# Attention and a Fourier mixer in one kernel on one core: the second product's additions spread over its pieces, forms of u in their own places, product with v behind the next step's scores

## The chip, the cores and the metric

The kernel runs on one core of a Trainium2 chip. A core has a matrix engine (TensorE, PE in the profile, with its weight loads listed as PEld), three engines for elementwise work (VectorE, DVE; ScalarE, ACT; GpSimd, POOL) and DMA queues, here issued by SyncE. Each engine works through its own queue of instructions, and semaphores tie the queues together. The metric is the device time of one launch in microseconds (us).

The profiler records one execution. Lines such as L1128 are lines of the kernel before; names such as `w_all` or `e` are those of its tiles.

## The reference

Two blocks follow each other. The first is attention with a threshold, for 8 batches of 8 heads, 576 rows, 64 columns a head:

```python
scores = scale * np.matmul(q, k.transpose(0, 1, 3, 2))
thresh = np.max(scores, axis=-1, keepdims=True) - tau
scores = np.where(scores >= thresh, scores, -1000000000.0)
scores = scores - np.max(scores, axis=-1, keepdims=True)
attn = np.exp(scores)
attn = attn / (np.sum(attn, axis=-1, keepdims=True) + 1e-09)
return np.matmul(attn, v)
```

The heads are put side by side, to x of 8 x 576 x 512, and the second block mixes it:

```python
mixed = np.real(np.fft.fft(np.fft.fft(x, axis=1), axis=2))
u = x + mixed
un = (u - mean(u)) / np.sqrt(var(u) + 1e-06)
ch = np.maximum(un @ w_ch1, 0.0) @ w_ch2        # 512 -> 2048 -> 512
return u + ch
```

Everything is float32.

## The kernel before

*Attention.* Two heads are handled together (a pair; 32 pairs in all, four to a batch). A pair takes five steps t = 0 to 4: four of 128 query rows for both heads and one for the 64 rows left over. In a step `scores` writes q times k to PSUM (tile `sc`, L427). `softmax` takes the negated row maximum on VectorE (L451), the exponential on ScalarE (L459), the threshold and the sum on VectorE (L467, then L472 and L481 on tiny columns) and normalizes one head's half of `e` on VectorE (L484) and the other on ScalarE (L488). In step t == 4 ScalarE then copies a corner of `e` (L497). One step later `weights_in_parts` transposes `e` on TensorE (`pe` at L530, `pw` at L548), and ScalarE copies the result to `e_t` (L550). `weighted_values` multiplies it with v (`pv`, L577), part 0 after step 2 and part 1 after the pair's last step.

*Mixing.* When the four pairs of a batch are there, `fold_rows` and `mixing` fold x by symmetry, go through two products with tables (`py` L680, `pa` and `pb` L697 to L705), and leave u, transposed, in `u_t`: L717 and L718 on VectorE, L720 and L724 on GpSimd.

*The two large products.* The 4608 rows are cut into nine groups of 512. Group 0 runs as plain products. Groups 1 to 8 run in `two_level`, which computes both products with Strassen-like schemes: seven products in place of eight, paid for with additions.
- The first product goes through four parts of seven products each, in the order `ORDER`. Its right operands are quarters of u or forms of them, t1 to t3 and minus_t4, each a subtraction of GpSimd (`u_form`, L997). Their four places come from the tile pool "u", which also holds the rows of u until the store of the result has read them.
- The second product applies the scheme on two levels. The outer loop runs over the seven products `L1`, the inner one over seven pieces `J`; each piece is four matmuls (eight records in the profile) into a bank (L1168), and after pieces 3 and 6 the bank is copied or added to a tile v_u, v_11, v_22, v_21 or v_12 (L1198, L1200, L1203). `l1_form` (L1090) and `l2_forms` (L1110) build the left operands one product ahead, on VectorE and GpSimd. At the end of outer product 7, one GpSimd addition (L1216, 128 x 1792) adds v_u to v_22 and v_21; `gather` (L1128) combines the seven columns of each by six calls; `finish` (L789) scales by 1/std and adds to u; then the rows are stored (L796). In this version all of that is emitted at one place, between two products. v_12 follows in the same manner after outer product 3, the last.

*Order of the work.* TensorE runs in the order of the program text. For the other engines, from the third batch on, the scheduler of the language orders the instructions. The main loop (L1490) goes through the attention steps: the scores of step i, then the transposes of step i-1 in two parts with `fill()` around them, then `softmax(i)`, then `fill()`, then `weighted_values`. `fill` draws one piece of mixing and as many pieces of the products as a budget of matmul columns allows; a group is a generator, and each `yield` ends a piece.

Of the kernel before, what the change touches and what calls it, by code (L numbers as in the profile page):

```python
# [9 lines left out]
FP32 = mybir.dt.float32  # L10
INT32 = mybir.dt.int32
UINT32 = mybir.dt.uint32
ALU = mybir.AluOpType
# [34 lines left out]
def kernel(  # L48
# [12 lines left out]
    nc = tc.nc  # L61
    B, H, S, D = q.shape
# [3 lines left out]
    NPAIR = H // 2  # L66
    NT = 5
    ND = DM // 128
# [9 lines left out]
    NG = B * S // BT  # L78
    RING = 2 * S

    const = ctx.enter_context(tc.tile_pool(name="const", bufs=1))
    sb = ctx.enter_context(tc.tile_pool(name="sb", bufs=2))
# [756 lines left out]

    ORDER = (1, 5, 2, 6, 4, 7, 3)
    L1 = (1, 2, 5, 4, 6, 7, 3)
    J = (1, 2, 5, 4, 6, 7, 3)
    HH = HID // 2
# [120 lines left out]
    s1_tile = w1[3]  # L966
    l2_room = [w2_all[:, 512 * n : 512 * (n + 1)] for n in range(6)]
    l2_at = 0
    NV = 7 * 128
    v_u, v_11, v_22, v_21, v_12 = (  # L970
        w2_all[:, 3072 + NV * n : 3072 + NV * (n + 1)] for n in range(5)
# [3 lines left out]
    def two_level(g, rows):  # L975
        forms = w2_forms() if g == 1 else iter(())

        def tokens(k, n):
# [6 lines left out]
            )  # L985

        b = {(k, n): tokens(k, n) for k in range(2) for n in range(2)}
        t1, t2, t3, minus_t4 = (
            sb.tile([128, 512], FP32, tag="u", bufs=4, name=f"t_u{m}")[:, :].rearrange(
                "p (c two n) -> p c two n", c=2, two=2  # L990
            )
            for m in range(4)
        )

        def u_form(out_, in0, in1):
# [30 lines left out]
        for part in range(4):  # L1026
# [4 lines left out]
            for at, m in enumerate(ORDER):  # L1031
# [37 lines left out]
                else:  # L1069
                    add(h01, bank[:, :])  # L1070
                    relu(h01, part == 3)
                next(forms, None)
                yield 4096
            if g > 1:
                s1_part(part)
        for _ in forms:
            pass
        if g == 1:
            for part in range(4):
                s1_part(part)  # L1080
# [4 lines left out]
        lefts = {}  # L1085

        def l1_form(out_, in0, in1, engines):
            for n, eng in enumerate(engines):
                c = slice(512 * n, 512 * n + 512)
                eng.tensor_tensor(out=out_[:, c], in0=in0[:, c], in1=in1[:, c], op=ALU.subtract)  # L1090

        def l2_forms(m):

# [16 lines left out]
                eng.tensor_tensor(out=out_, in0=in0, in1=in1, op=op)  # L1110
                yield

        def gather(eng, v, n):

            v = v.rearrange("p (v j n) -> p v j n", v=n, n=128)

            def at(first, count, step=1):
                return v[:, :, first : first + step * (count - 1) + 1 : step]

            def one(j, count):  # L1120
                base = v[:, :, j]
                return bass.AP(
                    tensor=base.tensor, offset=base.offset,
                    ap=[list(base.ap[0]), list(base.ap[1]), [0, count], [1, 128]],
                )

            def plus(to, other):
                eng.tensor_tensor(out=to, in0=to, in1=other, op=ALU.add)  # L1128

            for k in range(n):  # L1130
                w = v[:, k]
                p1 = bass.AP(
                    tensor=w.tensor, offset=w.offset, ap=[list(w.ap[0]), [0, 2], [1, 128]]
                )
                plus(w[:, 1:5:3], p1)
            plus(at(5, 1), at(4, 1))
            plus(at(6, 1), at(2, 1))
            plus(at(6, 1), at(4, 1))
            for k in range(n):
                w = v[:, k]  # L1140
                u3 = w[:, 5]
                u3 = bass.AP(
                    tensor=u3.tensor, offset=u3.offset, ap=[list(u3.ap[0]), [0, 2], [1, 128]]
                )
                plus(w[:, 2:4], u3)

        def finish(i, n, v):
            v = v.rearrange("p (j n) -> p j n", n=128)
            cols = slice(256 * n, 256 * n + 256)
            rows.add(2 * i, cols, v[:, 1:7:5])  # L1150
            second = v[:, 3:4]
            rows.add(2 * i + 1, cols, bass.AP(
                tensor=second.tensor, offset=second.offset,
                ap=[list(second.ap[0]), [-128, 2], [1, 128]],
            ))

        for _ in l2_forms(1):
            pass
        P, V = nc.gpsimd, nc.vector
        for at, m in enumerate(L1):  # L1160
            banks = []
            for jn, j in enumerate(J):
                if jn in (0, 4):
                    banks.append(ps.tile([128, 512], FP32, tag="mm", bufs=4, name="po"))
                to = banks[-1][:, 128 * (jn % 4) : 128 * (jn % 4 + 1)]
                right_ = block(g, True, 7 * at + jn)
                for s in range(4):
                    nc.tensor.matmul(  # L1168
                        to, lefts[m][j][:, s], right_[:, 128 * s : 128 * (s + 1)],
                        start=jn in (0, 4) and s == 0, stop=s == 3, skip_group_check=True,  # L1170
                    )
                if jn == 0:
                    if m == 4:
                        l1_form(s1_tile, s1_tile, a11, (V, P, V, P))
                    if m == 6:
                        l1_form(a12, a12, s1_tile, (V, P, V, P))
                    if at < 6:
                        coming = l2_forms(L1[at + 1])
                        next(coming)
                        next(coming)  # L1180
                    if m == 2:
                        l1_form(a21, a11, a21, (P, P, P, P))
                if jn in (2, 4) and at < 6:
                    next(coming)
                if jn == 3 and m in (2, 5, 4, 6):
                    rows.load({2: 2, 5: 3, 4: 0, 6: 1}[m])
                    if m == 6:
                        rows.factors()
                    yield ND * 128
                if jn in (3, 6):  # L1190
                    size = 512 if jn == 3 else NV - 512
                    src = banks[-1][:, 0:size]

                    def here(v):
                        return v[:, 0:512] if jn == 3 else v[:, 512:NV]

                    if m in (1, 5, 4):
                        nc.scalar.copy(here({1: v_u, 5: v_22, 4: v_21}[m]), src)  # L1198
                    elif m == 2:
                        V.tensor_tensor(out=here(v_11), in0=here(v_u), in1=src, op=ALU.add)  # L1200
                    else:
                        to = here(v_12 if m == 3 else v_u)
                        V.tensor_tensor(out=to, in0=to, in1=src, op=ALU.add)  # L1203
                if jn < 6:
                    yield 2048
            if m == 2:
                gather(P, v_11, 1)
            elif m == 6:
                P.tensor_tensor(out=v_12, in0=v_u, in1=v_22, op=ALU.add)
                finish(0, 0, v_11)  # L1210
            elif m == 7:
                twice = bass.AP(
                    tensor=v_u.tensor, offset=v_u.offset, ap=[list(v_u.ap[0]), [0, 2], [1, NV]]
                )
                both = v_22_21.rearrange("p (v n) -> p v n", v=2)
                P.tensor_tensor(out=both, in0=both, in1=twice, op=ALU.add)  # L1216
                gather(V, v_22_21, 2)
                finish(1, 1, v_22)
                finish(1, 0, v_21)
                rows.store(2)  # L1220
                rows.store(3)
            elif m == 3:
                gather(V, v_12, 1)
                finish(0, 1, v_12)
                rows.store(0)
                rows.store(1)
            background()
            yield 2048

    def settle(b):  # L1230

# [152 lines left out]
    def fold_more():  # L1384
        if folds and next(folds[0], True):
            folds.pop(0)
# [100 lines left out]
    by_hand.close()  # L1487
    ctx.enter_context(tc.manual_schedule(engines={mybir.EngineType.PE}))

    for i in range(2 * per_batch, total + 1):  # L1490


        if i < total:
            scores(i)
        n, t = divmod(i, NT)
        if t > 2:
            fold_more()
        weights = weights_in_parts(i - 1)
        if t == 1:
            prep_ends(n)  # L1500
        if t == 2 and n + 1 < B * NPAIR:
            scale_q(n + 1)
        if t == 3 and n + 1 < B * NPAIR:
            prep_pair(n + 1)
        fill()
        next(weights, None)
        fill()
        next(weights, None)
        if i < total:
            softmax(i)  # L1510
        fill()
        if t == 2:
            weighted_values(n, 0)
        if t == 0:
            while folds:
                fold_more()
            weighted_values(n - 1, 1)
            folds.append(fold_rows(n - 1))
            if n % NPAIR == 0:
                while folds:  # L1520
                    fold_more()
            if n + 1 < B * NPAIR:
                load_v(n + 1)
        if i % per_batch == 0:
            start_batch(i // per_batch - 1)
    per_slot = cost(0) / 40
    while mixes or work:
        fill()
# [46 lines left out]
```

## Time and profile before

Three runs took 1689.12 to 1691.37 us, with a median of 1690.09 us. The profiled execution spans 1689.9 us.

| Stretch of the span, us | TensorE busy | VectorE busy | ScalarE busy | GpSimd busy | Granted clock |
|---|---|---|---|---|---|
| 320 to 510 | 182.7 of 190 | 116.4 | 79.4 | 108.9 | 0.98 |
| 510 to 695 | 171.2 of 185 | 135.5 | 93.6 | 82.5 | 0.96 |
| 880 to 1064 | 174.5 of 184 | 136.9 | 93.7 | 84.2 | 0.97 |
| 1248 to 1433 | 175.9 of 185 | 135.2 | 94.7 | 83.0 | 0.97 |
| 1433 to 1690 | 231.6 of 257 | 127.9 | 52.4 | 122.7 | 0.96 |

Between 510 and 1433 us attention of the later batches and the groups of products run side by side; after 1433 us only the last mixing and the last products are left. The granted clock is the share of full speed at which TensorE was let run. Costly groups of instructions around the change, as busy time and mean length:

| Line | Engine, shape | Count | Busy us | Mean ns |
|---|---|---|---|---|
| L1041 first product | PE, 128x256 | 1792 | 431.5 | 386 |
| L1168 second product | PE, 128x128 | 3136 | 420.8 | 277 to 288 |
| L467 | DVE, 128x576 | 288 | 228.8 | 812 |
| L1128 `gather` | DVE, 128x256 and others | 96 | 46.5 | 550 |
| L1128 `gather` | POOL, 128x128 and others | 40 | 31.3 | 814 |
| L789 `finish` | DVE, 128x256 | 64 | 44.3 | 739 |
| L1216 | POOL, 128x1792 | 8 | 31.9 | 3982 |
| L1209 | POOL, 128x896 | 8 | 17.8 | 2222 |
| L997 forms of u | POOL, 128x256 | 64 | 48.6 | 767 to 788 |

A wait is read as follows: an engine's instruction is ready in its queue, and the profile names the instruction on another engine, or in its own queue, that released it last. A mean over a group can hide several cases, so the places themselves have to be looked at in order of time.

### The profile page before, as it was taken

Reading aid. Unit: us, or ns where it says so; the run is one execution under the profiler, and the core shown is the slowest. Engines: PE = TensorE matmul, PEld = TensorE weight load, DVE = VectorE, ACT = ScalarE, POOL = GpSimd, SP = SyncE. Lnnn points to the kernel's source line nnn. Section 1 sums busy time; section 2 is a strip of 40 time slices with the busy share of each in tenths; the row PEclk is TensorE's granted clock in tenths of the full one; section 3 lists DMA queues with packets and bytes.
Section 4 is the critical chain, followed back from the end, with each engine's and each line's share of the span. In section 5 each row is a group of like instructions: output and inputs, shape, how many; then the busy total and the mean of one; then the engine's idle time right before and its main releaser. Section 6 shows DMA issues by size and latency. Waiting matters only on the chain. (4 is left out here: it accounts for less than half of the span.)

```text
span 1689.9 us, 27055 instructions
## 1 busy us (share of the span) xinstructions
PE 1570.3 (93%) x9770; PEld 1213.6 (72%) x9770; DVE 1178.3 (70%) x2438; ACT 794.6 (47%) x1700; POOL 856.6 (51%) x953
## 2 busy tenths in 40 slices
PE   8998888998998899989999999899998999989997
PEld 4555444555786778777787678777877777879897
DVE  7987886546676767777677767876778767625546
ACT  5865665433544465445545464546545554222121
POOL 6784666357452634543362534453453426336436
PEclk9999999999999999999999999999999999999999
DMA  6343332445553434525353435433363425436655
GB/s 168 107 110 127 98 106 63 140 151 173 171 186 120 125 112 144 179 83 159 109 169 116 141 114 165 159 121 115 106 193 108 130 98 175 165 116 238 217 182 199
DMA packets 245499, 239.05 MB, mean 141 GB/s; under 512 B 196947, under 2 KB 214869, under 8 KB 225014
## 3 DMA queue, kind: packets, MB, share of 16 engines
q1 hardware_dynamic: 242854, 237.02, 45.2%
q8 instruction: 78, 1.28, 0.3%
q10 hardware_dynamic: 2512, 0.30, 0.1%
q14 instruction: 55, 0.45, 0.1%
HBM read 207.50 MB, written 29.62 MB: 140 GB/s over the span
## 5 line engine op out<-in xcount | busy, mean ns | idle before, releaser
L459 ACT ACTIVATE e<-sc,neg 128x576 f32<-128x576 f32 x288 | 211.8, 736 | 249.8 <-DVE neg L451 249.6
L451 DVE TENSOR_REDUCE neg<-sc 128x1 f32<-128x576 f32 x288 | 207.1, 747 | 130.2 <-PE sc L427 98.0
L467 DVE SCALAR_TENSOR_TENSOR e<-sc,thr,e 128x576 f32<-128x576 f32 x288 | 228.8, 812 | 47.9 <-ACT thr L463 46.6
L1041 PE MATMUL ph<-t_u,w 128*128 128x256 f32 x1024 | 245.5, 386 | 9.6 <-POOL t_u L997 9.3
L1168 PE MATMUL po<-w,w_all 128*128 128x128 f32 x1792 | 242.1, 288 | 5.9 <-ACT ends L540 5.3
L1168 PEld LDWEIGHTS po<-w,w_all 128*128 128x128 f32 x1792 | 226.9, 203 | 15.3 <-issue 7.8
L1041 PEld LDWEIGHTS ph<-t_u,w 128*128 128x128 f32 x1024 | 188.7, 192 | 42.9 <-POOL t_u L997 11.3
L1110 POOL TENSOR_TENSOR w_all<-hs 128x512 f32<-128x512 f32 x72 | 100.3, 1395 | 225.4 <-PE po L1168 122.9
L427 PE MATMUL sc<-kT,qT 64*128 64x288 f32 x1024 | 177.3, 434 | 25.8 <-DVE e L467 24.8
L1041 PE MATMUL ph<-u_t,w 128*128 128x256 f32 x768 | 186.0, 387 | 6.3 <-ACT hs L1052 5.6
L1010 DVE TENSOR_TENSOR hs<-ph,hs 128x512 f32<-128x512 f32 (+1 forms) x128 | 105.0, 821 | 114.3 <-PE ph L1041 114.3
L548 PE MATMUL pw<-ident,e 128*128 128x128 f32 x1152 | 172.8, 277 | 6.2 <-ACT u L769 2.9
L1041 PEld LDWEIGHTS ph<-u_t,w 128*128 128x128 f32 x768 | 143.9, 193 | 34.5 <-issue 8.6
L427 PEld LDWEIGHTS sc<-kT,qT 64*128 64x128 f32 x1024 | 96.1, 187 | 93.1 <-issue 39.5
L550 ACT COPY e_t<-pw 128x512 f32<-128x512 f32 x256 | 147.7, 590 | 30.5 <-PE pw L548 29.7
L548 PEld LDWEIGHTS pw<-ident,e 128*128 128x128 f32 x1152 | 138.4, 143 | 23.5 <-issue 5.7
L1022 POOL TENSOR_TENSOR w<-hs 128x512 f32<-128x512 f32 x32 | 40.6, 1269 | 216.2 <-ACT hs L1018 205.8
L1168 PE MATMUL po<-w,hs 128*128 128x128 f32 x960 | 128.7, 281 | 0.0
L1168 PEld LDWEIGHTS po<-w,hs 128*128 128x128 f32 x960 | 119.2, 196 | 5.9 <-issue 5.5
L488 ACT ACTIVATE e<-e,den 128x576 f32<-128x576 f32 x96 | 74.5, 776 | 66.7 <-DVE den L481 66.4
L1018 ACT ACTIVATE hs<-hs 128x512 f32<-128x512 f32 (+1 forms) x80 | 60.7, 758 | 78.7 <-DVE hs L1010 77.9
L484 DVE TENSOR_SCALAR e<-e,den 128x576 f32<-128x576 f32 x120 | 89.6, 747 | 3.7
(203 smaller groups left out, 2758.0 us busy)
## 6 DMA issues: line engine op xcount, KB each, us to landing
w<-f SPq DMA_DIRECT2D x152, 1024.0 KB, 4.9
hs<-in_moe_w_ch_dram SPq DMA_DIRECT2D x23, 512.0 KB, 4.6
q_in<-in_q_dram SPq DMA_DIRECT2D x128, 72.0 KB, 2.3
out_dram<-u SPq DMA_DIRECT2D x36, 256.0 KB, 2.3
k_in<-in_k_dram SPq DMA_DIRECT2D x124, 72.0 KB, 2.4
v_in<-in_v_dram SPq DMA_DIRECT2D x64, 128.0 KB, 2.4
f<-w SPq DMA_DIRECT2D x14, 512.0 KB, 4.9
f<-w SPq DMA_DIRECT2D x7, 1024.0 KB, 4.3
```

Of the source, the lines that this page charges most:

```text
L427: nc.tensor.matmul(sc[j][:, c, 0:HALF], qT[hp, 128 * t : 128 * t + 128], kT[hp, k0 + HALF * c : k0 + HALF * (c + 1)], start=True, stop=True,)
L451: nc.vector.tensor_reduce(out=neg[:, j : j + 1], in_=sc[j][:, :, 0:HALF], axis=AXIS_XY, op=ALU.max, negate=True,)
L459: nc.scalar.activation(out=ej, in_=sc[j][:, :, 0:HALF], func=ACT.Exp, bias=neg[:, j : j + 1], scale=1.0)
L467: nc.vector.scalar_tensor_tensor(out=ej, in0=sc[j][:, :, 0:HALF], scalar=thr[:, j : j + 1], in1=ej, op0=ALU.is_ge, op1=ALU.mult, accum_out ...
L484: nc.vector.tensor_scalar(out=e[:, 0:S], in0=e[:, 0:S], scalar1=den[:, 0:1], scalar2=None, op0=ALU.mult)
L488: nc.scalar.activation(out=e[:, S : 2 * S], in_=e[:, S : 2 * S], func=ACT.Copy, scale=den[:, 1:2])
L548: nc.tensor.transpose(pw[:, c, :], e[:, c0 : c0 + 128], ident[:, :])
L550: nc.scalar.copy(e_t[:, 4 * j : 4 * j + 4, qs], pw[:, :, :])
L1010: nc.vector.tensor_tensor(out=to, in0=bank, in1=to if other is None else other, op=ALU.add)
L1041: nc.tensor.matmul(bank[:, 256 * q : 256 * q + 256].rearrange("p (two n) -> p two n", two=2), left[:, 256 * c + 128 * q : 256 * c + 128 * ...
L1110: eng.tensor_tensor(out=out_, in0=in0, in1=in1, op=op)
L1168: nc.tensor.matmul(to, lefts[m][j][:, s], right_[:, 128 * s : 128 * (s + 1)], start=jn in (0, 4) and s == 0, stop=s == 3, skip_group_check ...
```

## The change

Four things are altered.

1. *Additions spread over the pieces.* The calls of `gather`, `finish`, `l1_form` and `l2_forms` become lists of single jobs. A table `side` gives each a slot (outer product, piece), and one or two of them are emitted after that piece. The addition of v_u to v_22 and v_21 becomes two of 128 x 896, after the first two pieces of the last outer product, and `gather(V, v_22)` and its `finish` follow in that product's later slots. What belongs to v_12 and v_21 goes into a list `pending`; `tick` takes two jobs from it after every product of the next group's first product. The last group empties it at once. `gather` now takes one tile of seven columns at a time, five calls each.
2. *Forms of u in places of their own.* For groups after the first, t1 has a tile of its own, and t2, minus_t4 and t3 lie in places of `l2_room`, the room of the left operands. The pool "u" then holds only rows of u.
3. *The order of the first product* changes from 1, 5, 2, 6 to 1, 2, 5, 6, so that the first form is needed one product later.
4. *Product with v behind the next scores.* `weighted_values`, the folding that hangs on it, `load_v` and `start_batch` move from the end of a step to behind the scores of the next step, ahead of its transposes.

The aim is that no engine's queue holds a long run of additions in front of an instruction that TensorE waits for, and that TensorE has work at hand while ScalarE copies `e_t`.

```diff
-    ORDER = (1, 5, 2, 6, 4, 7, 3)
+    ORDER = (1, 2, 5, 6, 4, 7, 3)
...
+    t1_room = const.tile([128, 512], FP32, name="t1_room")
...
-        t1, t2, t3, minus_t4 = (
-            sb.tile([128, 512], FP32, tag="u", bufs=4, name=f"t_u{m}")[:, :].rearrange(
...
+        else:
+            rooms = [t1_room[:, :]] + [l2_room[(l2_at + m) % 6] for m in (4, 5, 0)]
+        t1, t2, minus_t4, t3 = (
+            room.rearrange("p (c two n) -> p c two n", c=2, two=2) for room in rooms
         )
...
                 next(forms, None)
+                tick()
                 yield 4096
...
+        while pending:
+            tick()
...
+        side = {}
+
+        def at_slots(at, slots, jobs):
+            for jn, job in zip(slots, jobs, strict=True):
+                side.setdefault((at, jn), []).append(job)
...
+            at_slots(at, (1, 2, 3, 5) if at == 3 else (0, 1, 3, 5), [next_form] * 4)
+        coming = {}
+        at_slots(1, (1, 2, 4, 6), l1_form(a21, a11, a21, (P, P, P, P)))
+        at_slots(2, (4, 5, 6), l1_form(s1_tile, s1_tile, a11, (V, P, V, P))[0:3])
+        at_slots(3, (0,), l1_form(s1_tile, s1_tile, a11, (V, P, V, P))[3:4])
+        at_slots(4, (1, 2, 4, 6), l1_form(a12, a12, s1_tile, (V, P, V, P)))
+        at_slots(2, (0, 1, 2, 3, 4), gather(P, v_11))
+        at_slots(4, (0, 2), finish(0, 0, v_11))
+        at_slots(
+            5, (0,), [lambda: P.tensor_tensor(out=v_12, in0=v_u, in1=v_22, op=ALU.add)]
+        )
+        at_slots(6, (0, 1), [plus(P, v_22, v_u), plus(P, v_21, v_u)])
+        at_slots(6, (2, 2, 3, 4, 4), gather(V, v_22))
+        at_slots(6, (5, 5), finish(1, 1, v_22))
...
+                for job in side.get((at, jn), ()):
+                    job()
...
-            elif m == 7:
...
-                P.tensor_tensor(out=both, in0=both, in1=twice, op=ALU.add)
-                gather(V, v_22_21, 2)
-                finish(1, 1, v_22)
-                finish(1, 0, v_21)
-                rows.store(2)
-                rows.store(3)
-            elif m == 3:
-                gather(V, v_12, 1)
-                finish(0, 1, v_12)
-                rows.store(0)
-                rows.store(1)
...
+        pending.extend(gather(V, v_12))
+        pending.extend(gather(V, v_21))
+        pending.extend(finish(0, 1, v_12))
+        pending.append(stores(0, 1))
+        pending.extend(finish(1, 0, v_21))
+        pending.append(stores(2, 3))
+        if g == NG - 1:
+            while pending:
+                tick()
...
+        for _ in range(2):
+            if pending:
+                pending.pop(0)()
...
-    for i in range(2 * per_batch, total + 1):
+    for i in range(2 * per_batch, total + 2):
...
+        if t == 3:
+            weighted_values(n, 0)
+        if t == 1:
+            while folds:
+                fold_more()
+            weighted_values(n - 1, 1)
+            folds.append(fold_rows(n - 1))
...
+        if i % per_batch == 1:
+            start_batch(i // per_batch - 1)
...
         if i < total:
             softmax(i)
         fill()
-        if t == 2:
-            weighted_values(n, 0)
-        if t == 0:
-            while folds:
-                fold_more()
-            weighted_values(n - 1, 1)
-            folds.append(fold_rows(n - 1))
...
-        if i % per_batch == 0:
-            start_batch(i // per_batch - 1)
```

## The prediction

> **What bounds the kernel now.** I read the page's busy shares first, then the waits of TensorE, the list of its gaps in the timeline, and the granted clock in narrow windows around them.
>
> ```profile
> PE 1570.3 (93%) x9770; PEld 1213.6 (72%) x9770; DVE 1178.3 (70%) x2438; ACT 794.6 (47%) x1700; POOL 856.6 (51%) x953
> ```
>
> TensorE is busy for 93% of the span, so what a reordering can win is in the 120 us in which it is not, and in the time in which it runs slowly. Its waits over the whole span:
>
> ```profile
> PE sc L427 <- DVE e L467: 24.8, 25, 2.4
> PE pe L530 <- ACT e L497: 20.0, 6, 3.5
> PE pv L577 <- ACT e_t L550: 11.2, 11, 1.3
> ...
> PE ph L1041 <- POOL t_u L997: 9.3, 2, 5.5
> ...
> PE pa L697 <- DVE tmp L718: 3.6, 5, 1.1
> ```
>
> The columns are the total, how often, and the longest. In the timeline these waits repeat at fixed places: from 510 us to 1433 us the kernel goes through five rounds of 184.5 us (20 attention steps and about one group of rows each), and every full round has the same gaps: 1.0 us at pv, 2.37 us and 1.31 us at sc, 1.29 us at pv, 3.25 to 3.39 us at pe, 0.55 us or more at pa; together 9.8 us. The pe gap at 933.8 us, in order of time:
>
> ```profile
> 925.69 4.00 POOL L1216 TENSOR_TENSOR w_all<-w_all 128x1792 f32<-128x1792 f32 x1 [2.05 <-DVE w_all L1203]
> 929.72 4.59 DVE L1128 TENSOR_TENSOR w_all<-w_all 128x256 f32<-128x256 f32 x7 [2.36 <-POOL w_all L1216]
> 934.23 2.19 DVE L789 SCALAR_TENSOR_TENSOR u<-w_all,rstd,u 128x256 f32<-128x256 f32 x4
> 936.35 0.51 DVE L484 TENSOR_SCALAR e<-e,den 128x576 f32<-128x576 f32 x1
> 936.89 0.24 ACT L497 COPY e<-e 128x64 f32<-128x64 f32 x1 [1.50 <-DVE e L484]
> 937.19 0.47 PE L530 MATMUL pe<-ident,e 128*128 128x128 f32 x1 [3.39 <-ACT e L497]
> ...
> 941.08 4.33 PE L1168 MATMUL po<-w,w_all 128*128 128x128 f32 x24
> ```
>
> The reader is to see that L484, half a microsecond of work, stands in VectorE's queue behind eleven instructions of the second product, and these behind a 4.0 us addition of GpSimd. The same windows, with the granted clock third from the right:
>
> ```profile
> 931.00:934.00 3.00, 2.80 (x24) 2.61 (x23) 3.00 (x6) 0.00 (x0) 3.00 (x5) 1.00 0.76 311
> 934.00:937.00 3.00, 0.00 (x0) 0.00 (x0) 3.00 (x7) 0.51 (x2) 0.96 (x2) 1.00 0.01 5
> 937.00:940.00 3.00, 2.26 (x10) 1.44 (x11) 3.00 (x7) 2.54 (x7) 1.37 (x2) 0.53 0.64 195
> 940.00:943.00 3.00, 3.00 (x14) 2.29 (x13) 2.90 (x7) 1.13 (x3) 3.00 (x6) 0.50 0.01 3
> 943.00:946.00 3.00, 3.00 (x23) 2.63 (x24) 1.18 (x2) 0.00 (x0) 3.00 (x5) 0.83 0.33 49
> 946.00:949.00 3.00, 3.00 (x24) 1.63 (x22) 2.97 (x7) 0.42 (x1) 2.24 (x5) 1.00 0.86 347
> ```
>
> The last gap costs twice: TensorE idles 3.4 us and then runs at half clock. Summed over windows of 4 us, the clock missing after each such gap is 3.4 us; the 2.37 us gap is followed by 1.7 us missing, the gaps of 1.3 us and less by none.
>
> **What the skill says.** "TensorE: Matmul & The Clock Gate", Part 1 (the HAM clock gate): the clock drops to half after an idle window of about 3.4 us and comes back after about 3.4 us of activity. The trace agrees: 0.50 to 0.53 after 3.39 us of idleness, for about 6.8 us. The same page, under the array's architectural detail: ScalarE and VectorE queues are strict FIFO. The L484 lines agree. "GPSIMD Engine Reference", Specifications: GpSimd shares its SBUF interfaces with VectorE, and two-input instructions contend. The trace agrees: the 128x512 addition of L1110 on VectorE takes 0.69 us alone and up to 1.75 us beside GpSimd's additions.
>
> **The change, part by part.**
>
> *Product with v behind the next scores.* No instruction is added. Ahead of the scores the pv matmuls wait for the copy L550; behind them the copy is 1.2 us of sc further on and more, so the waits of 11.2 us go: +11.2. What the swap risks: sc now issues earlier by the pv block, 2.3 us (part 0) or 2.84 us (part 1), and needs L467 of the step before to be done. From the timeline, the distance from the end of the last L467 to sc at eight such places of one round is 3.3, 4.0, 6.2, 0.6, 7.3, 4.6, 5.3 and 4.6 us. Only the 0.6 is short, and it comes from fold and mixing work (L610 to L670) that stood between two L467s; in the queue built for the changed kernel both L451s and both L467s come ahead of it. So the 1.31 us wait shrinks to about 0.2: 5 x 1.1 = +5.5. VectorE also gets its scores 2.3 us sooner before the 2.37 us wait. There its queue is full from 866 to 881 us, after 1.56 us idle waiting for those very scores; I let the earlier start take 1.2 us off the wait and 1.2 of the 1.7 us of missing clock: 4 rounds x 2.4 = +9.6.
>
> *Additions one or two per piece.* Per group VectorE had 12 instructions at L1128 (two columns of v together) and gets 15 of single columns; five of these took 1.37 us at the end of the kernel, where GpSimd was idle, and 2.77 us at 946 us beside it. Three sets are 4.1 to 8.3 us against 47.8/8 = 6.0 us now: nothing either way. GpSimd's 4.0 us L1216 becomes two additions of 128x896, which L1209 prices at 2.2 us each, and the first half is enough for the first set. Counting from the scores of the last step of a pair (921.9 us): v_u is complete at 0.65 (one piece earlier than now, by the built order), GpSimd's first half ends at about 2.8, five additions end at 4.2 to 5.5, one L789 0.5, L467 0.8, one L789 0.5, L717 and L718 0.9, two additions 0.6, L472 and L481 0.3, L484 0.5: 8.3 to 9.6, and with L497 8.6 to 10.0. TensorE needs it after its 1.1 + 9.9 us of matmuls in between, at 11.0. The gap closes; I leave 0.3. Gain: 5 rounds x (3.3 - 0.3 + 3.0 of clock) = +30. The sixth wait of this kind, at 1432 us, is another: L1110 waits there for GpSimd ahead of L484, and the built order keeps that. Likewise the 5.3 us at 510 us.
>
> *The new wait.* The remaining additions, two transposes, two L789, two L451 and two L467 of the next step follow in the same queue, and end at 15.9 to 17.3 on the same scale. The scores after next, no longer behind pv, want to start at 15.4. I take 1.2 us, and 0.5 us for waits that I don't see: 5 x 1.7 = -8.5.
>
> *Forms of u in their own places, order 1, 2, 5, 6.* Eight additions of 0.72 us per group on GpSimd stay. Their wait for the store of u (26.3 us of GpSimd, 7 times) goes, and t1 is needed third, not second. Elsewhere nothing waited for them; TensorE did twice, near the end. At 1581.85 us it waited 3.73 us for t1, while GpSimd was idle for the stores, and 1.7 us of clock are missing after it: t1 can now be early, and t2 and minus_t4, whose places are read until the group before ends, have two further products of 1.9 us of cover: +5.4. At 1479.29 us it waited 5.54 us for t1 too, but there GpSimd was busy from 1474.7 to 1484.1 us with the mixing additions (L720, L724) that make the tokens t1 needs; the change gives that one more product of cover, 1.9 us, and the half clock behind it likely stays: +1.9. Together +7.3. Product 6 now directly follows 5, whose ScalarE copy VectorE needs: hidden by the eight matmul records of 6 ahead of its own addition (1792 of L1041 in eight groups of 28 products; 431.5 us in all, so 1.9 us a product) against a copy of 0.58 us.
>
> *The end.* Seven L1128 and four L789 behind L1216 now partly run beside the last matmuls: +1.3.
>
> Sum: 11.2 + 5.5 + 9.6 + 30 - 8.5 + 7.3 + 1.3 = 56.4 us, 1634 us. The low end of each unknown (L484's gap closed but for 1 us: 5 x (2.3 + 3.0); nothing off the 2.37 us wait; 3.5 us of new waits per round; nothing at the end) gives 11.2 + 5.5 + 26.5 - 17.5 + 7.3 = 33, 1657 us; with every gap named closed, clock included, and no new wait it is 11.2 + 6.5 + 16.4 + 33.5 + 7.3 + 1.3 = 76, 1614 us. VectorE is busy for 137 of the 184.5 us of a round now and would be for 78% of it then, so I lean to the slow side of the middle: 1638 us.
>
> **The rivals.** *The wait moves* (1658 us): scores that issue earlier catch VectorE at the place I called the new wait for over 3 us, so that the half clock returns there: 5 x 6.5 instead of 8.5 lost, 56.4 - 24 = 32. For it: 15.9 to 17.3 against 15.4 is close. Against: of the other seven places six have 0.4 us or more to spare once the pv block is taken off, most of them 1.7 to 4.5. *VectorE sets the pace* (no change, 1688 us): its 137 us per round are spread so unevenly that each gap closed opens another. Against: from 945 to 1044 us no gap over 0.4 us shows, at the same work per step. *Slower* (1720 us): two half-clock gaps per round (2 x 6.5 = 13), as one-column additions contend with GpSimd in new places, and waits of 0.8 us at all eight swaps (6.4): 19.4 lost against 11.3 won per round (the 56.4, without the 8.6 from the forms and the end and without the new wait), 5 x 8.1 = 40, less the 8.6. For it: everything repeats five times, mistakes too. Against: the spare time just listed.
>
> **How the numbers follow.** Forecast 0.68, wait moves 0.17, no change 0.03, slower 0.12. Faster 0.85, same 0.03, slower 0.12. The range runs from 1612 us, all gaps closed, to 1676 us, past the first rival with one more such place; it leaves out most of no change and slower.
>
> **What would show it.** Right: no pv wait on L550; no pe wait over 1 us but the one near 1400 us; t_u waits gone; clock at 1.00 all through a round but for one place at most. Wrong: new sc waits on L467 over 2 us once per round, with 0.5 clock after them; L1125 (as the additions are then numbered) still ahead of L484 with GpSimd's addition before it.

## The result, and the profile after

Three runs of the changed kernel took 1715.66 to 1719.02 us, with a median of 1717.22 us: 1.0160 of the time before, 95% interval 1.0137 to 1.0183. It is slower by 27 us (1.6%), where 52 us less was forecast.

```profile
PE 1574.0 (92%) x9770; PEld 1215.3 (71%) x9770; DVE 1199.5 (70%) x2462; ACT 795.0 (46%) x1700; POOL 854.3 (50%) x961
```

TensorE does the same work in the same busy time (1570.3 us before); its idle time grew. Its waits over the whole span, with the lines of the changed kernel (L1045 and L1195 are the two products' matmuls, L1001 the forms of u, L1121 the forms of the second product, L1125 the additions of `gather`; `ph` and `po` are the PSUM banks of the two products, `pn`, L763, that in which u is transposed back):

```profile
PE pe L530 <- ACT e L497: 23.8, 8, 4.8
PE pa L697 <- DVE tmp L718: 21.8, 5, 4.7
...
PE sc L427 <- DVE e L467: 9.1, 16, 1.7
PE pn L763 <- ACT x L583: 6.2, 5, 1.3
...
PE po L1195 <- ACT w_all L1207: 4.9, 4, 1.3
```

The reader is to see three things. The waits that the change aimed at are gone: pv no longer waits for L550 (11.2 us before), and the scores wait 9.1 us in place of 24.8. Two waits on ScalarE's copies out of PSUM, 6.2 us at pn and 4.9 us at po, are new. And the rounds have two kinds of gap over 4 us, where before they had one of 3.3 us.

The places were found in order of time, as before. A round now takes 191 to 194 us, not 184.5. From the first pa gap (563.82 us) to the fifth (1331.06 us), four rounds, there are 767.2 us, against 738.2 us from pe gap to pe gap before. TensorE's busy time in them is 702.9 against 697.6 us, its idle time 64.4 against 40.6 us: 23.8 + 5.3 = 29 us. The two profiled spans differ by 24.9 us, so the loss arises in the rounds. In all four rounds together:

| Gap of TensorE, released by | before, us | after, us |
|---|---|---|
| sc, L467 on VectorE | 14.7 | 0.8 |
| pv, L550 on ScalarE | 9.2 | 0 |
| pe, L497 on ScalarE | 13.1 (one per round) | 20.3 (one per round, at another place; a rest of 0.55 at the old one in three) |
| pa, L718 on VectorE | 3.1 | 17.6 |
| pn, po, pw, py and ph, on copies and sums of ScalarE and VectorE | 0.5 | 25.7 |

The waits that went (sc and pv, 23.1 us) and the small ones that came (25.2 us) nearly cancel; the two long gaps make the rest.

The first new gap, at 945.7 us, in order of time; here and below only the instructions that bear on a gap are shown:

```profile
943.23 2.68 DVE L1125 TENSOR_TENSOR w_all<-w_all 128x128 f32<-128x128 f32 x4
944.60 0.40 ACT L713 COPY tmp<-pa 128x289 f32<-128x289 f32 x1 [1.01 <-POOL u_t L720]
945.83 0.87 DVE L789 SCALAR_TENSOR_TENSOR u<-w_all,rstd,u 128x256 f32<-128x256 f32 x2
946.62 1.14 DVE L1125 TENSOR_TENSOR w_all<-w_all 128x128 f32<-128x128 f32 x4
947.68 0.48 DVE L789 SCALAR_TENSOR_TENSOR u<-w_all,rstd,u 128x256 f32<-128x256 f32 x1
948.08 1.42 DVE L451 TENSOR_REDUCE neg<-sc 128x1 f32<-128x576 f32 x2
949.41 0.45 DVE L717 TENSOR_TENSOR tmp<-pa,tmp 128x289 f32<-128x289 f32 x1
949.78 0.45 DVE L718 TENSOR_TENSOR tmp<-pa,tmp 128x289 f32<-128x289 f32 x1
950.37 0.64 PE L697 MATMUL pa<-seq_even,y_e 128*1 128x145 f32 x2 [4.67 <-DVE tmp L718]
```

L484, which the change was to free, ran ahead of all this. But the mixing's L717 had its input at 945.0 us, when L713 ended, and stood in VectorE's queue until 949.4 us, behind additions and L789s of the second product and then two row maxima (L451). TensorE needs L718 behind it.

The second, at 890.4 us:

```profile
877.18 4.84 POOL L1125 TENSOR_TENSOR w_all<-w_all 128x256 f32<-128x256 f32 x5 [1.29 <-DVE w_all L1209]
...
888.72 1.73 POOL L387 TENSOR_SCALAR q_in<-q_in,q_scale 128x576 f32<-128x576 f32 x1
...
891.00 2.48 POOL L1121 TENSOR_TENSOR w_all<-w 128x512 f32<-128x512 f32 x2
892.29 1.73 DVE L1121 TENSOR_TENSOR w_all<-w_all,w 128x512 f32<-128x512 f32 x1 [6.69 <-POOL w_all L1121]
...
894.32 0.52 DVE L484 TENSOR_SCALAR e<-e,den 128x576 f32<-128x576 f32 x1
...
895.17 0.47 PE L530 MATMUL pe<-ident,e 128*128 128x128 f32 x1 [4.81 <-ACT e L497]
```

VectorE stood idle for 6.69 us: its next instruction was s2 of outer product 6, and GpSimd was late with s1, which s2 needs (s1 and s2 are left operands that `l2_forms` builds one after the other, s1 as a sum, s2 as s1 less another tile). L484, whose exponentials were done at 885.6 us (L467), stood behind s2, with the two tiny instructions that it needs, L472 and L481. The granted clock after the first gap, third from the right:

```profile
950.00:954.00 4.00, 3.63 (x15) 2.49 (x16) 3.23 (x10) 2.41 (x6) 4.00 (x6) 0.50 0.15 60
954.00:958.00 4.00, 4.00 (x27) 3.44 (x25) 0.69 (x1) 0.00 (x0) 4.00 (x7) 0.78 0.11 19
```

In windows of 1 us, the clock missing with each of the five pa gaps and four pe gaps of the rounds adds up to 3.4 us (5.1 us with one of them). Before, it was 3.4 us with five gaps of 3.3 us and 1.7 us with four of 2.4 us.

### The profile page after: what moved, and what is told of

The parts are those of the page before. It is cut to its first block, busy times and chain, and to the rows that moved or that the text cites. A ratio compares the mean times of both kernels' runs of the same rounds, so it can differ in the third digit from the quotient of the medians.

```text
span 1714.8 us, 27077 instructions
## 1 busy us (share of the span) xinstructions
PE 1574.0 (92%) x9770; PEld 1215.3 (71%) x9770; DVE 1199.5 (70%) x2462; ACT 795.0 (46%) x1700; POOL 854.3 (50%) x961
## 4 chain that ended last, share of the span: by engine, by line
PE 55%; DVE 24%; POOL 10%; ACT 5%; issue 4%; DMA 2%; SPq 0%; DVEq 0%; ACTq 0%; POOLq 0%
PE ph L1045 20%; PE po L1195 10%; PE pv L577 6%; PE sc L427 6%; PE pw L548 4%; DVE e L467 4%; DVE w_all L1125 3%; DVE neg L451 3%; PE po L821 3%; DVE w_all L1121 2%; POOL w_all L1125 2%; PE ph L803 2%; ACT e L459 2%; POOL w_all L1121 1%; DMA w<-f 1%
## 5 line engine op out<-in xcount | busy, mean ns | idle before, releaser
L459 ACT ACTIVATE e<-sc,neg 128x576 f32<-128x576 f32 x288 | 211.7, 735 | 277.5 <-DVE neg L451 277.2
L451 DVE TENSOR_REDUCE neg<-sc 128x1 f32<-128x576 f32 x288 | 206.3, 746 | 117.5 <-PE sc L427 98.3
L467 DVE SCALAR_TENSOR_TENSOR e<-sc,thr,e 128x576 f32<-128x576 f32 x288 | 228.9, 814 | 57.2 <-ACT thr L463 56.2
L1195 PE MATMUL po<-w,w_all 128*128 128x128 f32 x1792 | 246.7, 292 | 9.4 <-ACT w_all L1207 4.9
L1195 PEld LDWEIGHTS po<-w,w_all 128*128 128x128 f32 x1792 | 231.1, 207 | 21.6 <-issue 9.9
L1121 POOL TENSOR_TENSOR w_all<-hs 128x512 f32<-128x512 f32 x72 | 97.8, 1359 | 227.4 <-PE po L1195 152.2
L548 PE MATMUL pw<-ident,e 128*128 128x128 f32 x1152 | 174.0, 278 | 20.5 <-ACT ends L536 5.3
L1045 PE MATMUL ph<-u_t,w 128*128 128x256 f32 x768 | 181.5, 382 | 4.3 <-ACT x L583 1.9
L550 ACT COPY e_t<-pw 128x512 f32<-128x512 f32 x256 | 148.7, 593 | 49.2 <-PE pw L548 48.4
L548 PEld LDWEIGHTS pw<-ident,e 128*128 128x128 f32 x1152 | 137.4, 143 | 41.9 <-ACT ends L536 8.4
L1045 PEld LDWEIGHTS ph<-u_t,w 128*128 128x128 f32 x768 | 140.8, 190 | 30.8 <-issue 8.2
L1045 PE MATMUL ph<-w_all,w 128*128 128x256 f32 x672 | 158.6, 383 | 1.5 <-DVE hs L1014 1.5
L1045 PEld LDWEIGHTS ph<-w_all,w 128*128 128x128 f32 x672 | 123.1, 190 | 23.6 <-issue 5.8
L1195 PE MATMUL po<-w,hs 128*128 128x128 f32 x960 | 127.2, 279 | 1.9 <-ACT ends L536 1.4
L1195 PEld LDWEIGHTS po<-w,hs 128*128 128x128 f32 x960 | 117.5, 194 | 7.9 <-issue 5.1
L484 DVE TENSOR_SCALAR e<-e,den 128x576 f32<-128x576 f32 x120 | 90.2, 751 | 3.5
```

What stands on the lines that cost most here:

```text
L451: nc.vector.tensor_reduce(out=neg[:, j : j + 1], in_=sc[j][:, :, 0:HALF], axis=AXIS_XY, op=ALU.max, negate=True,)
L459: nc.scalar.activation(out=ej, in_=sc[j][:, :, 0:HALF], func=ACT.Exp, bias=neg[:, j : j + 1], scale=1.0)
L467: nc.vector.scalar_tensor_tensor(out=ej, in0=sc[j][:, :, 0:HALF], scalar=thr[:, j : j + 1], in1=ej, op0=ALU.is_ge, op1=ALU.mult, accum_out ...
L484: nc.vector.tensor_scalar(out=e[:, 0:S], in0=e[:, 0:S], scalar1=den[:, 0:1], scalar2=None, op0=ALU.mult)
L548: nc.tensor.transpose(pw[:, c, :], e[:, c0 : c0 + 128], ident[:, :])
L550: nc.scalar.copy(e_t[:, 4 * j : 4 * j + 4, qs], pw[:, :, :])
```

## The experiments

The first four runs set two theories against each other: 'additions', that the additions in their new slots make both long gaps, and 'swap', that scores issued earlier make them. From e5 on the theory is 'queue order': instructions that TensorE waits for stand, at two or three places per round, behind others in the queues of VectorE and ScalarE. Its rival is 'throughput': VectorE and GpSimd are short of time in these stages, so that a wait that is taken away turns up at the next place. Ratios are to the kernel before on the same chip, with their 95% intervals.

| Run | What it is | Median, us | Ratio |
|---|---|---|---|
| changed | all four alterations | 1717.2 | 1.0160 [1.0137, 1.0183] |
| e1 | before + swap of pv and scores | 1726.5 | 1.0195 [1.0175, 1.0215] |
| e2 | before + places of u and order | 1708.3 | 1.0086 [1.0066, 1.0107] |
| e12 | before + places of u, old order | 1707.1 | 1.0063 [1.0039, 1.0088] |
| e3 | changed - swap | 1709.3 | 1.0094 [1.0068, 1.0120] |
| e4 | changed - spread additions | 1755.4 | 1.0368 [1.0349, 1.0387] |
| e5 | changed, s1 on VectorE | 1689.3 | 0.9993 [0.9983, 1.0004] |
| e6 | changed, additions behind L718 | 1703.5 | 1.0078 [1.0063, 1.0093] |
| e7 | changed, both | 1672.9 | 0.9902 [0.9885, 0.9918] |
| e15 | e7 + one copy ahead | 1663.9 | 0.9845 [0.9830, 0.9860] |
| e8 | e3, additions behind L718 | 1706.8 | 1.0102 [1.0086, 1.0117] |
| e9 | e1 + copies ahead at every step | 1739.3 | 1.0257 [1.0239, 1.0275] |
| e10 | e9 + s1 on VectorE | 1735.7 | 1.0238 [1.0217, 1.0258] |
| e11 | e7 + copies ahead at every step | 1721.8 | 1.0150 [1.0131, 1.0169] |
| e13 | e1 + copy ahead at one step | 1735.3 | 1.0262 [1.0245, 1.0280] |
| e14 | e13 + s1 on VectorE | 1705.5 | 1.0085 [1.0069, 1.0101] |
| e16 | before + s1 on VectorE | 1684.7 | 0.9955 [0.9942, 0.9969] |
| e17 | e1, L789 behind L451 | 1711.9 | 1.0109 [1.0087, 1.0132] |
| e18 | e17 + s1 on VectorE | 1683.5 | 0.9942 [0.9920, 0.9963] |

### Which part loses

**e1, the swap alone.** The main loop of the changed kernel in the kernel before.

> The kernel before with the fourth alteration alone (product with v behind the next step's scores). Theory 'additions' (VectorE's and GpSimd's additions in their new slots stand ahead of L718 and L484 and make the two new gaps of 4 to 5 us): the pv waits on L550 (11.2 us) go, the pe gap of 3.3 us and its half clock stay, neither new gap appears; 1665 to 1680 us. Theory 'swap' (scores that issue earlier shift the attention steps against VectorE's other work, and this alone makes the new gaps): a gap over 4 us at pa or at pe in every round, 1700 us or more.

**e2, the places of u with the order 1, 2, 5, 6 alone; e12, the places with the old order.** The line in which e12 (+) differs from e2 (-):

```diff
-    ORDER = (1, 2, 5, 6, 4, 7, 3)
+    ORDER = (1, 5, 2, 6, 4, 7, 3)
```

> The kernel before with the forms of u in places of their own and the order 1, 2, 5, 6 alone. Both theories: no new gaps; t1 no longer waits for stores near 1582 us; 1680 to 1688 us.

> The second run (forms of u in their own places and order 1, 2, 5, 6; 1708 us) with the old order 1, 5, 2, 6: the places alone. If the order of the first product carries the loss of 15 us: 1680 to 1692 us. If the places do (GpSimd's forms run as soon as the tokens are there, and the scheduler orders VectorE's queue anew around them): 1700 to 1712 us.

**e3, the changed kernel with the main loop of before; e4, the changed kernel with the second product of before.**

> The changed kernel with the product with v put back to the end of the step: additions spread and forms of u stay. Theory 'additions': both gaps of 4 to 5 us stay and the pv waits come back, 1720 to 1735 us. Theory 'swap': the new gaps go and the pe gap stays closed, 1655 to 1675 us.

> The changed kernel with the additions of the second product put back into lumps between the products: swap and forms of u stay. Theory 'additions': the sum of the first two runs, 1660 to 1675 us, with the pe gap of 3.3 us once per round. Theory 'swap': as slow as the changed kernel or slower, 1705 us or more.

Measured: the swap alone loses 2.0%, the places with the order 0.9%, swap, places and order together 3.7%. 'Additions' had e1, e2 and e4 faster than the kernel before and falls. 'Swap' had e1 and e4 right, but not e3, where it expected both gaps gone and a time of 1655 to 1675 us; and neither theory had e2's loss. Putting the additions into slots, which 'additions' held guilty, is worth 2.0% on top of the other two (1.0368 to 1.0160), and nothing without the swap (1.0086 to 1.0094). The traces divide the gaps: the pa gap of 4.1 us is in e3, without the swap, and not in e1, so the spread additions make it; the pe gap of about 5 us is in e1 and e4, without the spread, and at most 2.3 us in the rounds of e3, so the swap makes it. In e1 the old pe gap stays too (2.9 us), and there is another, 4.1 us at py, in the place where pv stood:

```profile
919.23 2.46 POOL L1209 TENSOR_TENSOR w_all<-w_all 128x896 f32<-128x896 f32 x1 [2.50 <-DVE rstd L782]
919.67 2.69 DVE L789 SCALAR_TENSOR_TENSOR u<-w_all,rstd,u 128x256 f32<-128x256 f32 x2
922.29 1.41 DVE L451 TENSOR_REDUCE neg<-sc 128x1 f32<-128x576 f32 x2
923.11 1.28 ACT L459 ACT_TABLE_LOAD   x1 [3.47 <-DVE neg L451]
...
925.04 0.58 ACT L550 COPY e_t<-pw 128x512 f32<-128x512 f32 x1
925.67 0.56 PE L680 MATMUL py<-dim_c,f 128*48 128x65 f32 x3 [4.10 <-ACT e_t L550]
```

L550 had its input at 919.8 us. It stood in ScalarE's queue behind L459, L459 waited for L451, and L451 stood on VectorE behind two L789, slowed by GpSimd's L1209. Before the swap the same chain ended in the 1.29 us wait at pv.

The places of u seem to lose more than the order: 0.6% of the 0.9%, but the intervals of e2 and e12 overlap. In e2 the wait of the forms for the store is down from 26.3 us to 4.9 us. But VectorE's additions took longer. The group of `gather` on VectorE in e2:

```profile
L1132 DVE TENSOR_TENSOR w_all<-w_all 128x256 f32<-128x256 f32 (+1 forms) x96 | 59.4, 683 | 25.1 <-POOL w_all L1220 24.9
```

It was 46.5 us for the same 96 instructions, and VectorE's busy time as a whole rose from 1178.3 to 1217.8 us. A reading of this is that GpSimd, freed of the wait, now runs beside these additions and slows them; whether that or the scheduler's new order carries the loss was not tried.

### The two gaps of the changed kernel

**e5, s1 of outer product 6 on VectorE.**

```diff
-                (V if m == 1 else P, s1, x21, x22, ALU.add),
+                (V if m in (1, 6) else P, s1, x21, x22, ALU.add),
```

> The changed kernel, with one thing altered: the first addition of l2_forms for outer product 6 (s1, L1121) runs on VectorE, not on GpSimd, so that VectorE's next form s2 doesn't wait for GpSimd ahead of L484. Theory 'queue order': the pe gap of 4.5 to 4.8 us (four rounds) shrinks under 1.5 us and the half clock behind it goes, 4 x (3.3 + 3.4) = 27 us: 1685 to 1697 us; the pa gap on L718 stays. Rival 'throughput' (VectorE and GpSimd together are short of time in this stage, and TensorE meets the same lack at the next place): the gap turns up at po or sc with the same size, 1710 to 1720 us.

**e6, the additions of v_22 into the pending list, and that list behind the latest L718** (`issue_after` prescribes an order in one engine's queue and adds no wait for the result).

```diff
-        at_slots(6, (2, 2, 3, 4, 4), gather(V, v_22))
-        at_slots(6, (5, 5), finish(1, 1, v_22))
...
+        pending.extend(gather(V, v_22))
+        pending.extend(finish(1, 1, v_22))
...
-                pending.pop(0)()
+                with tc.issue_after(behind[0]):
+                    pending.pop(0)()
```

> The changed kernel, with VectorE's additions of the last outer product (gather and finish of v_22) put at the head of the pending list, and everything in that list queued behind the latest L718 on VectorE. Theory 'queue order': the pa gap of 4.1 to 4.7 us on L718 shrinks under 1 us in all five rounds with its half clock, 5 x (3.6 + 3.4) = 35 us: 1677 to 1692 us. Rival 'throughput': the additions, now later, stand before the softmax of the first product's steps, sc or pe waits of the same sum arise there, 1708 to 1720 us.

**e7, both; e8, the deferral without the swap.**

> The changed kernel with both alterations (s1 of product 6 on VectorE, additions behind L718). Theory 'queue order': the gains add up, 1650 to 1668 us, below the kernel before. Rival 'throughput': 1700 us or more.

> The changed kernel with the product with v back at the end of its step, and the additions queued behind L718. Theory 'queue order': the third run (1709 us) less its pa gap of 4.1 us and the half clock, 5 x 7 = 35: 1670 to 1682 us. Rival 'throughput': 1700 us or more.

e5 measured what 'queue order' said: the pe gap is gone in its trace (1.5 to 1.7 us at sc or po are left of it), and the ratio falls by 1.7%. e6 gave 0.8% where 2% was expected. Its pa gap is gone, but in each round a gap of 3.3 to 4.6 us stands a little later; the rival had foretold one, though at sc or pe. In e7, where it is the same, the chain is:

```profile
933.09 4.14 DVE L1125 TENSOR_TENSOR w_all<-w_all 128x256 f32<-128x256 f32 x5
937.15 1.41 DVE L451 TENSOR_REDUCE neg<-sc 128x1 f32<-128x576 f32 x2
937.93 0.74 ACT L459 ACTIVATE e<-sc,neg 128x576 f32<-128x576 f32 x1 [9.97 <-DVE neg L451]
939.42 0.41 ACT L583 COPY x<-pv 128x320 f32<-128x320 f32 x1
...
939.89 0.95 PE L548 MATMUL pw<-ident,e 128*128 128x128 f32 x4 [4.61 <-ACT x L583]
```

The additions, now later, hold L451; L459 waits for it; and the copy L583, whose input was there at 932.3 us, waits behind L459. The two edits together are worth 2.6%, and the kernel is then 1.0% faster than the one before, though 5 us slower than 'queue order' expected at most. e8 gained nothing: without the swap the deferral moves the wait as 'throughput' said (gaps of 6.0 to 6.2 us at the transposes pw in three rounds of its trace).

**e16, s1 on VectorE in the kernel before.**

> The kernel before with s1 of outer product 6 on VectorE. It tells whether this alteration is a gain of its own or mends what the change brought in. In the kernel before, VectorE waited only 1.67 us for GpSimd there and TensorE had a wait of 2.37 us at the next scores with 1.7 us of missing clock, four times. If it is a gain of its own: 1672 to 1682 us; if it mends the change only: 1686 to 1694 us.

It gave 0.45%, between the two expectations. So of the 1.7% of e5 about a quarter could be had without the change; the rest mends it. The quarter does not come from the gap at the scores, which grew from 2.37 to 3.07 us in all four rounds. In the trace two waits outside them got shorter: 5.27 to 3.34 us at po (515 us), and 3.52 to 2.21 us at pe (1437 us).

### ScalarE's copies

**e9, e10, e11: the exponentials behind the first L550 and L583 at every step.**

```diff
+            with ExitStack() as ahead:
+                for done in copied:
+                    ahead.enter_context(tc.issue_after(done))
+                softmax(i)
```

> The first run (swap alone, 1726 us), with one order of ScalarE's queue prescribed: the exponentials of a step (L459) stand behind the copies out of PSUM that the step emitted before them, the first L550 and L583. In the swap alone these copies stood behind L459, which waited for VectorE, and TensorE waited 4.1 us for their bank. Theory 'queue order': that gap and its half clock go, 5 x 7.5 = 37 us: 1684 to 1697 us; the pe gap of 5.2 us stays. Rival 'throughput' (the engines are short of time there, TensorE meets the lack at the next place): 1715 us or more.

> The same, with s1 of outer product 6 on VectorE too. Theory 'queue order': the pe gap of 5.2 us (four rounds) shrinks under 1.5 us with its half clock, another 4 x 7 = 28 us off: 1655 to 1672 us, so that the swap alone, with two queue orders mended, is a gain. Rival 'throughput': 1690 us or more.

> The run with both alterations (1673 us), with the copies L550 and L583 ahead of L459 as well. There the last gap of a round, 3.3 to 4.6 us at the first product or the transposes, ended with L583. Theory 'queue order': it goes with its half clock, 5 x (3.0 + 3.2) = 31 us at best: 1640 to 1655 us. Rival 'throughput': VectorE's pending additions ahead of L451 still hold the step, 1665 us or more.

All three missed what 'queue order' expected and came out as 'throughput' had them. The py gap is gone in e9, but the scores wait 67.0 us in all for L467 (8.7 us in e1), up to 6.5 us at once: prescribed at every step, the order costs more than the one gap. s1 on VectorE brings only 0.2% in e10; the pe wait of e9 was 2.9 us, not 5.2, and stays.

**e13, e14: the same at one step per round; e15: one copy, L583, ahead in e7.**

```diff
+        if i < total and t == 2 and n % NPAIR == 0:
+            with tc.issue_after(copied[0]):
+                softmax(i)
```

> The first run (swap alone) with the ScalarE order prescribed at one place of a round only: in the step t == 2 of a batch's first pair, where TensorE waited 4.1 us for the bank of L550, the step's exponentials stand behind the first L550 of the transposes before them. The prescription at every step had closed that gap, and opened others. Theory 'queue order': the gap goes with its half clock and nothing else moves, 5 x 7.5 = 37 us less than the first run's ratio of 1.0195 to the kernel before, a ratio of 0.994 to 1.002. Rival 'throughput': the wait turns up at the following scores, a ratio over 1.012.

> The same with s1 of outer product 6 on VectorE too, which took 28 us off the changed kernel. Theory 'queue order': both gaps go, a ratio of 0.975 to 0.988: the swap is then a gain, as its removed waits of 11.2 us and more say. Rival 'throughput': a ratio over 1.0.

> The run with both alterations (ratio 0.990) with one more order of ScalarE's queue: in the step t == 1 of a batch's second pair, where TensorE waited 3.3 to 4.6 us for L583, the exponentials stand behind L583. Theory 'queue order': a ratio of 0.971 to 0.980. Rival 'throughput' (VectorE's additions still hold this step's softmax, the next scores wait in place of the transposes): a ratio of 0.987 to 0.993.

e13 held with the rival: the gap of 4.1 us at py became one of 3.5 us at the next scores, for L467, and the time rose by 0.7%. VectorE is late there, and ScalarE's queue only hands it on. e14 is 1.8% better than e13 by s1 alone, which repeats e5 without the spread; its ratio over 1.0 is still the rival's. e15 lies between the two expectations: 0.6% better than e7. Its remaining gap is 1.8 us in three of five rounds, and 3.5 and 4.1 us in the others, where a sum on VectorE (L1212) took the place of the copy.

**e17, e18: is VectorE late by the order or by the amount of its work?** `finish(0, 0, v_11)` moves behind the maxima of the step (the lines of this kernel are two higher: L453 is L451, L791 is L789, L550 is L548).

```diff
-                finish(0, 0, v_11)
...
+                if jn == 3 and m == 7:
+                    with tc.issue_after(maxima[0]):
+                        finish(0, 0, v_11)
```

> The first run (swap alone, ratio 1.0195) with two pairs of instructions exchanged in VectorE's queue, once per round: the two L789 of outer product 6 stand behind the two L451 of the same place, not ahead of them. L789 took 2.7 us there beside GpSimd's L1209, and L451, ScalarE's exponentials, the copy L550 and TensorE waited for it in turn (gap of 4.1 us). Theory 'VectorE's queue is the cause and ScalarE's order only hands it on': the gap falls to about 1.4 us and the half clock goes, 5 x (2.7 + 3.4) = 30 us, a ratio of 1.000 to 1.006. Rival 'throughput' (as when ScalarE's order was prescribed, the next scores wait instead, since L467 comes no earlier): a ratio of 1.012 or more.

> The same with s1 of outer product 6 on VectorE. If both gaps that the swap opened are mended by these two alterations of order, a ratio of 0.980 to 0.990; if the lateness only moves on, 0.995 or more.

```profile
915.00 1.41 DVE L453 TENSOR_REDUCE neg<-sc 128x1 f32<-128x576 f32 x2
915.83 1.28 ACT L461 ACT_TABLE_LOAD   x1 [1.48 <-DVE neg L453]
916.34 1.36 DVE L791 SCALAR_TENSOR_TENSOR u<-w_all,rstd,u 128x256 f32<-128x256 f32 x2
918.08 0.66 PE L550 MATMUL pw<-ident,e 128*128 128x128 f32 x4 [1.61 <-ACT ends L538]
```

The gap fell from 4.1 to 1.6 us, as expected, so the order of these four instructions made it. The time fell by 0.9%, half of what was expected; the ratio of 1.0109 lies between the two expectations, and its interval takes in the rival's bound of 1.012. The two profiled spans tell where the sum was too high (17 us less, 30 expected). TensorE's idle time fell by 9.4 us, not by the 12.5 of the five gaps, since the scores waited 4.0 us more. The clock missing over the span fell by 14.6 us, but TensorE's busy time by 7.6 only: the sum had taken each us of missing clock for one us of time.

With s1 as well the ratio is 0.9942, just short of the rival's bound, which its interval takes in. That is no better than s1 without the swap (0.9955, the intervals overlap): with both of its gaps mended, the swap is worth nothing that these runs can tell. Neither theory holds throughout. An order mended at one place brought all or part of its sum in e5, e6, e15 and e17; in e8, e9 to e11 and e13 the wait turned up elsewhere.

## Why the prediction was wrong

**The waits of pv and scores** were right in their mechanism: the pv waits went, and the scores' waits in the rounds went almost wholly, 14.7 to 0.8 us. The failed part is to have booked them as won: 25.2 us of small waits came in at pn, po, pw, py and ph. That these are the old waits handed on isn't shown, and for po it does not fit: its 1.2 to 1.3 us stand right behind the pe gap, and e2, without the swap, has 5.4 us there.

**The L484 gap** closed to 0.55 us or less, near the 0.3 us that the step left.

**"The new wait"** is the first step that failed. I listed what stands in VectorE's queue after L484 and asked only when the scores need L467. L717 and L718 of the mixing's second half are queued there too, and TensorE comes to them before it comes to the scores. The step had 8.5 us for five rounds; the pa waits took 21.8 us, with the half clock besides. The line for it was in the profile before: pa waited for L718 five times, 3.6 us in all. e3 has this gap without the swap, e1 and e4 without the spread additions have not, and in e6, where the additions stand behind L718, it is gone.

**The 2.37 us wait** is the second. I took it for VectorE's, as the profile names L467, and let the swap win 9.6 us on it. But in those 16 us before (866 to 882 us) GpSimd was busy for 15.5 us, and at their end VectorE's s2 waited for it:

```profile
882.74 0.69 DVE L1110 TENSOR_TENSOR w_all<-w_all,w 128x512 f32<-128x512 f32 x1 [1.67 <-POOL w_all L1110]
```

In the changed kernel TensorE reached pe before GpSimd had made s1: 4.5 to 4.8 us, four times, with the half clock. e5 shows that this addition on GpSimd makes the gap, since moving it to VectorE closed it and brought 28 us. That the short wait at the scores had given GpSimd its time is a reading; e3 fits it, where a round has either 2.4 us at the scores (and at most 0.7 us at pe) or 2.3 us at pe. No step of mine followed GpSimd's queue.

**"Additions: nothing either way"** was mis-sized: `gather` on VectorE took 69.4 us for 120 instructions, against 46.5 us for 96. Four single-column additions took 2.68 us beside GpSimd and 1.14 us without it (the lines at 943.23 and 946.62 us).

**Forms of u** were priced at +7.3 us and cost 0.6 to 0.9% alone. The gap at 1479 us fell by 1.2 us (1.9 predicted), and that of t1 at 1581 us went. Not asked was what GpSimd and the queues would do once the wait for the store was gone.

**The rival "slower"** came near: 1720 us, and two half-clock gaps in four of five rounds. In part this is luck: its waits at all eight swaps did not come, and contention shows in the additions' times, but not as the maker of either gap. What I had against it, the spare time ahead of the scores (at all seven places by its own figures, not six), was true and not to the point: the instructions that became late were not the ones that I measured.

The Trainium skill's "TensorE: Matmul & The Clock Gate", architectural detail, says that ScalarE and VectorE queues are strict FIFO. The prediction applied it to one instruction. The traces agree: VectorE's queue stood for 6.69 us with L484 behind its head, and in e7 the copy L583 went 7 us after its input was there, behind L459. On the clock the prediction let the trace agree with the same page too readily: its own windows show the half clock for about 6.8 us, where it had quoted about 3.4 us of activity.

Open is what the places of u cost by contention and what by the new order of VectorE's queue, and why a us of missing clock cost only about half a us in e17.

## What to carry to other kernels

When a wait is taken away, list everything behind the mended place in each queue that it touches, with the moment at which another engine needs each; the first of them that is late sets the gain, and it need not be the one that the waits named before. A short wait of the fastest engine may be what keeps a slower one in step, so follow that engine's queue too. And mend the engine that is late, not the queue that hands the lateness on: one order of ScalarE's copies prescribed at every step cost 0.6% to 2.5% here, and at one place lost 0.7% (e13) or won 0.6% (e15). One addition moved off a late engine brought 1.7% to 1.8% where TensorE's gap hung on it, and 0.2% to 0.45% where it did not.

## What the runs showed of the hardware

- Two L789 (128x256) took 2.69 us beside GpSimd's addition of 128x896 and 0.87 us without it.
- The 2.37 us gap was followed by 1.7 us of missing clock, and gaps of 3.3 us by 3.4 us. With gaps of 4.1 to 5.2 us part of the half clock falls into the gap itself (a clock of 0.76 in e1's 922 to 926 us, where TensorE was busy for 0.33 us), and behind the pe gaps a further gap of 1.2 us stands inside it. So the clock's cost and the idle time overlap, and adding them up overstates the gain from closing such a gap.
- ScalarE's table load took 1.28 us ahead of the exponential, after the square root of L779, and stood in the chain of the py gap.
